# A spectral mixing block and a SwiGLU block under adaptive LayerNorm: a new order in the prologue, other PSUM banks for the last row transform, corrections by side copies, and the gate broadcast moved into the row loop

## The chip, the cores and the metric

The kernel runs on one core of a Trainium2 chip. A core has five engines with instruction queues of their own, each worked off in order: TensorE (PE, matrix products; its weight loads are listed as PEld), VectorE (DVE), ScalarE (ACT), GpSimd (POOL) and SyncE (SP, which here only issues DMAs). PE writes its results to PSUM, eight banks of 512 float32 in each of 128 partitions; DVE and ACT read them there. DMAs are issued from SP's, ACT's or POOL's queue. The metric is the device time of one execution in microseconds (us). A measurement is the median of several runs.

## The reference

One batch of 2048 rows (S) and 640 columns (D), in bfloat16. The model vector c gives six vectors of 640 through silu(c) @ w_mod: shift sa, scale ca and gate ga of the first half, sb, cb and gb of the second.

```python
def _A_ref(x, w_r, w_i):                     # spectral mixing
    X = rfft2(x, axes=(-2, -1))              # over rows and columns
    X = X * (w_r + 1j * w_i)
    return irfft2(X, s=(S, D)).astype(bfloat16)

def _B_ref(x, w_gate, w_up, w_down):
    return silu(x @ w_gate) * (x @ w_up) @ w_down      # inner width 1728

mod = (silu(c) @ w_mod).reshape(1, 6, 1, -1)
sa, ca, ga, sb, cb, gb = (mod[:, i] for i in range(6))
h = layernorm(x) * (1 + ca) + sa
x = x + ga * _A_ref(h, w_r, w_i)
h = layernorm(x) * (1 + cb) + sb
x = x + gb * _B_ref(h, w_gate, w_up, w_down)
```

## The kernel before

**Order.** The program is written in the order in which each engine is to run it; there is no scheduler. An engine that waits holds up all that stands behind it in its queue. SP's queue of DMAs is one list as well.

**Prologue (to about 15 us).** x comes in tiles of 128 rows, two (T = 2t, 2t + 1) to each of eight steps t. The column transform needs tables R (`Rp`, scaled by 1 + ca to `Rs`), the row transform tables `Gtab`. `bn(T)` takes mean and variance on DVE (two statistics instructions and an aggregate), `bn_act(T)` on ACT (two passes); `BA` (L341) lists the tiles that ACT takes. `rstd_of(t)` forms the variances on DVE (`vtmp`) and has POOL raise them to the power -1/2; `normed(t)` writes the two normalized tiles on DVE. `mod_cols` on PE gives ca, from which DVE forms `one_p_ca` and `m4c` and then, with POOL and ACT, the eight rows of `Rs`. `idle_pe` runs matmuls whose result is not used. `fetch(n)` issues n of 16 gathers from POOL's queue; they bring rows of the spectral weights w_i, w_r in reversed order into `Wt`.

**Row loop (L473, 15 to 38 us).** For each step, `tok(t)` multiplies the normalized tiles by `Gtab` (token product, banks 0 to 2), ACT copies the result (`Ys`), and `ddft(t)` multiplies it by `Rs` (banks 3 to 6); ACT copies that into `A_sb`. DVE and POOL prepare later steps meanwhile. At t = 5 `sa_cols`, at t = 7 `sa_rows` give the transform of the shift sa, and `sa_fix` its corrected form `FSA`, inside ddft(7). The copies of ddft(7) are split between DVE and ACT.

**Groups (38 to 69 us).** The 81 complex columns l are worked in 21 groups of up to four: 48 to 63 (groups 0 to 3), then {0, 80} (4), 1 to 47 (5 to 16), 64 to 79 (17 to 20). Groups 0 to 4 are transposed on PE (`t2_pe`), the others by four DMA transposes on SP (`t2_dma`). In each transposed block one column, index 0, needs a correction: `fix_in` multiplies it by the table TF, and DVE adds `FSA`. Then per group:
- `stage_a`: a PE product with KS2 per column, then two DVE products (`prod`, L574) with the spectral weights, for which `wsum` on POOL or DVE has formed a sum;
- `stage_b`: PE adds and transposes, ACT copies to `Y2`;
- `stage_c`, for units of one to three groups: PE multiplies by the inverse table KI; ACT (twice DVE) evicts into `Em` (columns below 64) or `Er`.

Index 0 of the second half is special again: for group 4 and the last six groups `row_col` has POOL copy it to `Zc`, and `stage_c` runs a second full matmul per column with KD. For the other columns `Y2c` collects index 0, and `row0` (L594) multiplies it by KI0, has ACT copy it (`E0c`) and SP store it into row 0 of `Em` by two small DMAs. Among the groups stand also the remaining model vectors: `ga_mod` (ga, broadcast to all partitions, `ga_bc`), and `mod_col` (sb, cb, gb; 25 matmuls of one column each), whose weights come by SP behind the transposes.

**Output rows (69 to 87 us).** For each of 16 tiles `s1em` and `s1er` on PE, a copy to `VT` on ACT, a PE product with RI (multiplied by ga; L1172, L1175), and on DVE the sum with x (`x1`, L1177). The second LayerNorm begins here: for the first two tiles `ln2_xn`, a DMA transpose on SP (`ln2_tr`, L777) and `ln2_mod` on POOL (L785), which applies cb and sb. The FFN weights come by SP, behind the two stores of row0: w_down (L722), two small pieces, then w_gate and w_up (L734). `gu13` (L989), the first product of the FFN, is on PE ahead of the last output tile.

**FFN (87 us to the end).** Four chunks of tiles, gate and up (L1001, L1031), then down (L879, L902).

Of the kernel before, what the change touches and what calls it, by code (L numbers as in the profile page):

```python
# [18 lines left out]
NT, P = 16, 128  # L19
# [68 lines left out]
def _tables():  # L88
# [28 lines left out]
    K = np.zeros((128, 832))  # L117
# [7 lines left out]
    K[:, 512:640] = C0 - Cr  # L125
# [48 lines left out]
def adaln_block_kernel(ctx, tc, A_x, A_w_r, A_w_i, B_x, B_w_gate, B_w_up, B_w_down, c, w_mod, out):  # L174
# [24 lines left out]
    Ktab = const.tile([P, 832], BF16, name="Ktab")  # L199
    KS2, KI, KB = Ktab[:, 0:192], Ktab[:, 192:320], Ktab[:, 320:384]  # L200
    TF, KD, KI0 = (Ktab[:, 384 + 128 * i:512 + 128 * i] for i in range(3))
    KDB = Ktab[:, 768:832]
    modcols = const.tile([P, 4, NC5], F32, name="modcols")
# [20 lines left out]
    FSA = const.tile([P, NL], F32, name="FSA")  # L224
# [9 lines left out]
    wm_r = rM.cut(12800, [NC5, 4, D])  # L234
# [14 lines left out]
    Zc = [rY.cut(4096 + 1024 * i, [4, 128]) for i in range(3)]  # L249
# [22 lines left out]
    nc.scalar.dma_start(Gtab[:, 0:2], Gd[:, 0:2])  # L272
    def load_x(xl, xh, gl, gh):
        nc.sync.dma_start(xh_sb[:, :, xl:xh, :], x_v[:, :, xl:xh, :])
        nc.sync.dma_start(Gtab[:, gl:gh], Gd[:, gl:gh])
# [4 lines left out]
    load_x(2, 3, 2, 6)  # L280
    nc.sync.dma_start(Rp[:, 0:4], R_dram[:, 0:4])
# [57 lines left out]
    if True:  # L339
        CS = (4, 0, 1, 2, 3)  # L340
        BA = (1, 3, 5, 11)  # L341

        def bn(T):
            for k in range(2):
                nc.vector.bn_stats(bn6a[:, k, :], x_sb[:, xslot(T), 320 * k:320 * k + 320])
            nc.vector.bn_aggr(mv[:, T, :], bn6a[:])
# [5 lines left out]
        def rstd_of(t):  # L352
            ts = slice(2 * t, 2 * t + 2)
            if 2 * t + 1 in BA:
# [6 lines left out]
            nc.gpsimd.tensor_tensor(rstd[:, ts], vtmp[:, ts], mhalf[:, 0:2], ALU.pow)  # L361

        def normed(t):
            for h in range(2):
                T = 2 * t + h
                nc.vector.tensor_scalar(XN[t % 3][h][:], x_sb[:, xslot(T), :], mv[:, T, 0:1], rstd[:, T:T + 1],
                                        ALU.subtract, ALU.mult)
# [14 lines left out]
        def ddft(t, mid=()):  # L382
            Ys = YS[t % 3]
            for ck in range(2):
                dft_d(banks(3 + 2 * ck, 2, [4, 256]), [Ys[:, CS.index(c5), 128 * ck:128 * ck + 128] for c5 in range(NC5)])
                if mid:
                    mid.pop(0)()
            for m in mid:
                m()
            Av = A_sb[:, :, t].rearrange("p l k c r -> p k c l r")  # L390
            av = banks(3, 4, [8, 256])[:, :, 0:RC].rearrange("p (k r) (c l) -> p k c l r", k=2, c=2)
            if t < NS - 1:
                nc.scalar.copy(Av, av)
            else:
                for ls in (slice(48, 64), slice(0, 48), slice(64, 81)):
                    for ck, cp in ((0, nc.vector.tensor_copy), (1, nc.scalar.copy)):
                        cp(Av[:, ck, :, ls], av[:, ck, :, ls])

        cps = psum[:, 7, 500:500 + NC5]
# [14 lines left out]
        fetch(2)  # L414
        bn(0)
        bn_act(1)
        rstd_of(0)
        bn(2)
        bn_act(3)
        fetch(1)  # L420
        normed(0)
        idle_pe(4)
        mps = psum[:, 7, 0:32 * NC5]
# [3 lines left out]
        idle_pe(3)  # L427
        mps = mps.rearrange("p (c w) -> p c w", w=32)[:, :, 0]
        rstd_of(1)
        nc.vector.tensor_scalar_add(one_p_ca[:], mps, 1.0)  # L430
        bn_act(5)
        nc.vector.tensor_scalar_mul(m4c[:], mask4[:], one_p_ca[:, 4:5])
        tok(0)
        for r in (1, 3):
            nc.scalar.mul(Rs[:, 0, r, :], Rp[:, r, :], one_p_ca[:, r:r + 1])
        normed(1)
        for r in range(2, 4):
            nc.gpsimd.tensor_scalar(Rs[:, 1, r, :], Rp[:, 4, :], m4c[:, r:r + 1], 1.0, ALU.mult, ALU.mult)
        for r in range(2):
# [3 lines left out]
        bn(4)  # L443
        fetch(1)
        rstd_of(2)
        fetch(2)
        bn(6)
        normed(2)
        idle_pe(2)

        def sa_cols():
            mps = psum[:, 7, 431:431 + NC5]
# [8 lines left out]
        def sa_rows():  # L461
            sps = psum[:, 7, 431:431 + NL]
# [5 lines left out]
        def sa_fix():  # L468
            fps = psum[:, 7, 431:431 + NL]
            nc.tensor.matmul(fps, lhsT=TF, rhs=SAb[:], start=True, stop=True)  # L470
            nc.vector.tensor_copy(FSA[:], fps)

        for t in range(1, NS):  # L473
            tok(t)
            if t < 6:
                (bn_act if 2 * t + 5 in BA else bn)(2 * t + 5)
                rstd_of(t + 2)
                if t < 5:
                    bn(2 * t + 6)
                normed(t + 2)  # L480
                fetch(1 + t % 2)
            ddft(t - 1)
            if t == 5:
                sa_cols()
                fetch(16)
            if t == 7:
                sa_rows()
        ddft(7, [sa_fix])
# [6 lines left out]
    if True:  # L495
        B2of = {}

        def t2_dma(bi):
# [4 lines left out]
            for i in range(n):  # L503
                B2of[l0 + i] = (B2b, i, l0, n)

        t2_dma(0)
        t2_dma(1)
        t2_dma(2)
        t2_dma(3)
        nc.sync.dma_start(wm_r[:, :, 1:3, :], wm_m[:, :, 1:3, :])  # L510
        nc.sync.dma_start(wm_r[:, :, 3, :], wm_m[:, :, 3, :])
# [3 lines left out]

        def fix_in(B2, n, fx, parts):
            nc.tensor.matmul(fx, lhsT=TF, rhs=B2[:, 0:n, 0], start=True, stop=True)
            for i0, i1, ls in parts:
                nc.vector.tensor_tensor(B2[:, i0:i1, 0], fx[:, i0:i1], FSA[:, ls], ALU.add)

        def t2_pe(slot):
            ls = groups[slot] + (groups[4] if slot == 3 else [])
            n = len(ls)
            tp = banks((0, 1, 6, 7)[slot], 1, [8, 128], BF16)
            for i, l in enumerate(ls):
                nc.tensor.transpose(tp[:, i, :], A_sb[:, l].rearrange("p t k c r -> p (t k c r)"), identb[:])
            B2 = (rM.cut(38400 + 1024 * slot, [n, 128]) if slot < 2 else rM.cut(10240 + 1024 * (slot - 2), [n, 128]))
            nc.scalar.copy(B2[:], tp[:, :n, :])
            for i, l in enumerate(ls):
                B2of[l] = (B2, i, None, None)  # L530

        def t2_fix(slot):
            B2, n = B2of[groups[slot][0]][0], 6 if slot == 3 else 4
            l0 = groups[slot][0]
# [775 lines left out]
```

## Time and profile before

| | us |
|---|---|
| median of 3 runs (lowest, highest) | 253.84 (253.65, 254.29) |
| the profiled execution's own time | 254.42 |
| its span, first to last instruction | 252.6 |
| to 10 us: PE busy | 5.83 of 10 |
| 10 to 38: PE, ACT, POOL busy | 24.00, 21.76, 20.04 of 28 |
| 38 to 69: PE, DVE, ACT busy | 28.91, 25.07, 23.88 of 31 |
| 69 to 87: PE busy | 17.82 of 18 |
| 87 to 253: PE busy | 162.21 of 166 |

A line of the timeline gives the start and the busy time in us, the engine (a q behind it stands for its queue, which issues a DMA), the line of the kernel, the operation, what it writes and reads with its shape, and how many instructions are merged. In brackets stands the time for which the engine was idle just before, and what ended that wait. A line of the windows gives a stretch of time, for each engine the busy time and the number of instructions, the granted PE clock (1.00 is full), the mean busy share of the DMA engines and GB/s. A line of the waits says who waited for whom: us in total, times, longest.

### The profile page before, as it was taken

How to read it: one execution, taken by the hardware profiler on the slowest of the kernel's cores; microseconds unless marked ns; L12 is line 12 of the kernel's file. 1: busy time of each engine (PE TensorE's matmuls, PEld its weight loads, DVE VectorE, ACT ScalarE, POOL GpSimd, SP SyncE). 2: the span in 40 equal slices, each digit the busy share in tenths (PEclk: the TensorE clock that was granted, in tenths of full speed). 3: DMA queues.
4: the chain of work that ended last, by engine and by line, in shares of the span. 5: the costliest groups of instructions: out<-in, count | busy, mean ns of one | idle time of the engine just before them, and what ended most of it. 6: DMA issues, size and time to landing. Idle time of an engine off the chain costs nothing.

```text
span 252.6 us, 5944 instructions
## 1 busy us (share of the span) xinstructions
PE 238.8 (95%) x2240; PEld 186.5 (74%) x2240; DVE 202.3 (80%) x493; ACT 171.1 (68%) x327; POOL 76.5 (30%) x111
## 2 busy tenths in 40 slices
PE   7587887999999999999999999999999999999994
PEld 2366866899989888778887778888675666656773
DVE  3695827997669999698998996778998788779964
ACT  5379876898689788858965387876247777774220
POOL 6675788671060633102001320000442000003410
PEclk9689999999999999999999999999999999999999
DMA  7999418998899999910001420300511000000111
GB/s 179 370 380 327 150 42 155 150 346 307 252 302 298 349 277 229 207 33 4 0 3 36 84 61 31 56 0 4 104 52 55 0 0 0 4 0 1 55 52 52
DMA packets 41310, 31.61 MB, mean 125 GB/s; under 512 B 22017, under 2 KB 37954, under 8 KB 41154
## 3 DMA queue, kind: packets, MB, share of 16 engines
q1 hardware_dynamic: 38704, 25.45, 36.9%
q0 software_dynamic: 2144, 5.58, 8.9%
q10 hardware_dynamic: 434, 0.21, 0.5%
q8 instruction: 17, 0.28, 0.5%
q14 instruction: 11, 0.09, 0.1%
HBM read 23.91 MB, written 2.62 MB: 105 GB/s over the span
## 4 chain that ended last, share of the span: by engine, by line
PE 83%; ACT 5%; DMA 3%; POOL 3%; DVE 2%; issue 2%; SPq 1%; DVEq 0%; ACTq 0%
PE psum L1031 35%; PE psum L902 19%; PE psum L1001 6%; PE psum L879 3%; DMA rM<-in_w_mod_dram 3%; PE psum L653 3%; PE psum L581 3%; PE psum L551 2%; PE psum L1172 2%; PE psum L1175 2%; PE psum L989 2%; POOL rW L336 2%; PE psum L377 1%; ACT rY L584 1%; PE psum L621 1%
## 5 line engine op out<-in xcount | busy, mean ns | idle before, releaser
L1031 PEld LDWEIGHTS <-rW 128*128 128x128 bf16 (+1 forms) x429 | 42.0, 98 | 12.6
L1031 PE MATMUL psum<-rW 128*128 128x256 bf16 (+1 forms) x247 | 42.2, 287 | 0.0
L928 POOL TENSOR_TENSOR rM<-rM,rL 128x320 f32<-128x320 f32 x6 | 5.4, 907 | 96.6 <-ACT rL L927 96.6
L902 PEld LDWEIGHTS <-rE 128*128 128x128 f16 (+1 forms) x196 | 19.0, 97 | 7.8
L902 PE MATMUL psum<-rE 128*128 128x320 f16 (+1 forms) x147 | 22.9, 299 | 0.0
L574 DVE TENSOR_TENSOR rM<-psum,rW 128x384 bf16<-128x384 f32 (+2 forms) x42 | 20.6, 547 | 2.1 <-PE psum L551 1.4
L1069 ACT COPY rX<-psum 128x384 f32<-128x384 f32 (+2 forms) x27 | 14.0, 519 | 7.3 <-PE psum L1031 7.2
L1062 ACT COPY rH<-psum 128x384 f32<-128x384 f32 (+2 forms) x27 | 13.9, 517 | 7.3 <-PE psum L1031 6.5
L1031 PEld LDWEIGHTS <-rE 128*128 128x128 f16 x156 | 15.2, 98 | 4.8
L1066 DVE TENSOR_TENSOR rH<-psum,rM 128x512 bf16<-128x512 f32 (+1 forms) x24 | 15.0, 624 | 4.4 <-PE psum L1031 2.6
L1085 ACT ACTIVATE rL<-psum 128x384 bf16<-128x384 f32 (+2 forms) x27 | 14.4, 532 | 5.4 <-PE psum L1031 3.4
L1070 DVE TENSOR_TENSOR rX<-psum,rX 128x384 f32<-128x384 f32 (+2 forms) x27 | 16.3, 604 | 1.7 <-ACT rX L1069 1.4
L1056 ACT COPY rM<-psum 128x384 f32<-128x384 f32 (+2 forms) x27 | 13.9, 515 | 4.0 <-PE psum L1031 3.9
L1031 PE MATMUL psum<-rE,rY 128*128 128x256 f16 (+1 forms) x78 | 15.6, 290 | 0.0
L1031 PE MATMUL psum<-rW,rE 128*128 128x256 bf16 (+1 forms) x78 | 15.6, 290 | 0.0
L1177 DVE SCALAR_TENSOR_TENSOR rM<-psum,rX 128x640 f32<-128x640 f32 x16 | 13.1, 821 | 2.7 <-ACT rL L657 1.4
L1086 ACT ACTIVATE rL<-rX 128x384 bf16<-128x384 f32 (+2 forms) x27 | 15.1, 558 | 0.0
L584 ACT CAST rY<-psum 128x512 bf16<-128x512 f32 (+2 forms) x21 | 11.8, 574 | 4.1 <-PE psum L581 3.7
L1001 PE MATMUL psum<-rW 128*128 128x256 bf16 x130 | 14.5, 273 | 0.0
L871 DVE TENSOR_TENSOR rA<-psum,rM 128x320 bf16<-128x320 f32 (+1 forms) x27 | 12.1, 472 | 2.4 <-PE psum L879 2.3
L1001 PEld LDWEIGHTS <-rW 128*128 128x128 bf16 x130 | 12.7, 98 | 1.6 <-issue 0.2
L1074 DVE TENSOR_TENSOR rH<-psum,rH 128x384 bf16<-128x384 f32 (+1 forms) x21 | 12.9, 615 | 0.0
(213 smaller groups left out, 641.7 us busy)
## 6 DMA issues: line engine op xcount, KB each, us to landing
out_dram<-rA SPq DMA_DIRECT2D x31, 80.0 KB
rM<-in_w_mod_dram SPq DMA_DIRECT2D x3, 800.0 KB
rA<-in_B_w_down_dram SPq DMA_DIRECT2D x2, 960.0 KB
rY<-in_B_w_gate_dram POOLq DMA_DIRECT2D x2, 832.0 KB
rM<-in_w_mod_dram SPq DMA_DIRECT2D x1, 1600.0 KB
rX<-in_A_x_dram SPq DMA_DIRECT2D x4, 320.0 KB
rX<-in_A_x_dram SPq DMA_DIRECT2D x2, 640.0 KB
rW<-in_B_w_gate_dram SPq DMA_DIRECT2D x2, 640.0 KB
```

Source lines behind the costliest of these rows:

```text
L574: nc.vector.tensor_tensor(PP[:, :, hl], xv[:, :, hl], in1, ALU.mult)
L584: nc.scalar.copy(Y2[:, 0:n, :], yps[:, 0:n, :])
L902: nc.tensor.matmul(o, lhsT=lhs[rows(k), k], rhs=rhs[rows(k), k], start=start and k == ks[0], stop=stop and k == ks[-1], skip_group_check=True)
L1001: nc.tensor.matmul(gu[u], lhsT=Wgu[:, u, c5, ff * 128:(ff + 1) * 128], rhs=h2T[:, :, c5, :], start=(c5 == 0), stop=(c5 == NC5 - 1))
L1031: nc.tensor.matmul(o[:, f], lhsT=w, rhs=b, start=(start and f == 0 and i == 0), stop=(stop and f == len(groups[g]) - 1 and i == len(ops) - ...
L1056: nc.scalar.copy(c0, X)
L1062: nc.scalar.copy(c2, X)
L1066: nc.vector.tensor_tensor(c11, Z, c0, ALU.add)
L1069: nc.scalar.copy(c3, X)
L1070: nc.vector.tensor_tensor(c22, Y, c3, ALU.add)
L1085: nc.scalar.activation(g21, X, ACT.Silu, scale=-1.0)
L1086: nc.scalar.activation(g22, c22, ACT.Silu, scale=-1.0)
```

## The change

**Prologue.** Tile 0's and tile 1's variances are formed and raised to the power separately. tok(0) goes ahead of ca's `mod_cols`, which stands behind it. `BA` is cut to tiles 1 and 3; DVE takes tiles 5 and 11. DVE's order becomes: normed(1), bn(4), one_p_ca, Rs, bn(5). In SP's queue Rp's four rows and two tiles of Gtab go ahead of the third x load. POOL forms no row of Rs any more, writes `sc_rep` at the start, and issues its gathers in a new order: one before tok(0), four behind, two before the loop, then two, two, two and three in steps 1 to 4. `fetch(3)` at t = 5 finds none left.

**Row loop.** bn and normed change their order and distance. `ddft` uses banks 4 to 7, and for t = 7 banks 0 to 3; the copies of ddft(6) are split between DVE and ACT as well. At t = 7 DVE forms `wsum` of columns 48 to 63, and the two `ga_mod` run on PE around ddft(6), with their copies on DVE. `sa_rows` stands behind ddft(7); `sa_fix` and `FSA` go.

**Groups.** The correction of index 0 adds the shift inside PSUM, by a second matmul with TF. For the blocks transposed on PE, DVE copies index 0 to a side tile `Bc` first, and ACT copies the rest. Group 5 is transposed on PE as well. For the blocks from the DMA transposes the correction runs two groups ahead, and ACT copies it back, behind the products. `Zc`, its memset and `row_col` go: the second matmul of `stage_c` writes only output partition 0, and for groups 17 and 18 `col0` corrects index 0 by two small matmuls with KM and an ACT copy, so that they need no second matmul. sb, cb and gb are formed at groups 14, 16 and 18, 25 matmuls each, and `row0` at group 19, with two ACT copies. The last two units run ahead of `s1em(0)` and `s1em(1)`. `wsum` on POOL is earlier. `wm_r` is laid out with the vector outermost, and its last three parts are loaded one by one.

```diff
-    K = np.zeros((128, 832))
+    K = np.zeros((128, 960))
...
-    K[:, 512:640] = C0 - Cr
+    K[:, 512:640] = C0 @ np.linalg.inv(Cr)
+    K[:, 832:960] = C0 - Cr
...
+    KM, KD = KD, Ktab[:, 832:960]
...
+    nc.sync.dma_start(Rp[:, 0:4], R_dram[:, 0:4])
+    nc.sync.dma_start(Gtab[:, 2:4], Gd[:, 2:4])
...
-    load_x(2, 3, 2, 6)
-    nc.sync.dma_start(Rp[:, 0:4], R_dram[:, 0:4])
+    load_x(2, 3, 4, 6)
...
-        BA = (1, 3, 5, 11)
+        BA = (1, 3)
...
-        def ddft(t, mid=()):
+        def ddft(t):
             Ys = YS[t % 3]
+            zb = [banks(4 + 2 * ck, 2, [4, 256]) for ck in range(2)]
+            if t == NS - 1:
+                zb = [banks(0, 2, [4, 256]), banks(2, 2, [4, 256])]
             for ck in range(2):
-                dft_d(banks(3 + 2 * ck, 2, [4, 256]), [Ys[:, CS.index(c5), 128 * ck:128 * ck + 128] for c5 in range(NC5)])
...
+                dft_d(zb[ck], [Ys[:, CS.index(c5), 128 * ck:128 * ck + 128] for c5 in range(NC5)])
...
+        def ga_mod(lo, bank):
+            gps_ = mod_bc(0, lo, bank)
+            nc.vector.tensor_copy(ga_bc[:, :, lo // 4:lo // 4 + 80], gps_.rearrange("p (m r) -> p r m", r=4))
+
+        def mods(i, mps):
+            for c5 in range(NC5):
+                mod_col(mps[:, c5:c5 + 1], wm_r[:, :, i], c5)
+            if i == 2:
+                return lambda: nc.vector.tensor_scalar_add(one_p_cb[:], mps, 1.0)
+            return lambda: nc.vector.tensor_copy(modcols[:, 2 + i // 2, :], mps)
...
         nc.gpsimd.memset(SL[:], 0.0)
-        fetch(2)
+        nc.gpsimd.tensor_copy(sc_rep[:], sc_f[:].unsqueeze(2).to_broadcast([P, NC5, 128]))
         bn(0)
+        rstd_of(0, 0)
         bn_act(1)
-        rstd_of(0)
-        bn(2)
+        bn(2, True, False)
+        rstd_of(0, 1)
+        fetch(1)
+        normed(0, (0,))
+        bn(2, False, True)
+        normed(0, (1,))
         bn_act(3)
-        fetch(1)
-        normed(0)
-        idle_pe(4)
-        mps = psum[:, 7, 0:32 * NC5]
+        idle_pe(6)
+        tok(0)
+        rstd_of(1)
+        fetch(4)
+        mps = psum[:, 3, 0:32 * NC5]
         mod_cols(mps, wm_ca, range(0, 3), 32)
         idle_pe(1, 2)
         mod_cols(mps, wm_ca, range(3, 5), 32)
-        idle_pe(3)
+        idle_pe(2)
         mps = mps.rearrange("p (c w) -> p c w", w=32)[:, :, 0]
-        rstd_of(1)
+        normed(1)
+        bn(4)
         nc.vector.tensor_scalar_add(one_p_ca[:], mps, 1.0)
-        bn_act(5)
...
-        tok(0)
...
+        bn(5)
         rstd_of(2)
         fetch(2)
-        bn(6)
-        normed(2)
-        idle_pe(2)
...
         for t in range(1, NS):
             tok(t)
             if t < 6:
-                (bn_act if 2 * t + 5 in BA else bn)(2 * t + 5)
+                bn(2 * t + 4)
+            if t < 7:
+                normed(t + 1)
+            if t < 6:
+                bn(2 * t + 5)
                 rstd_of(t + 2)
                 if t < 5:
-                    bn(2 * t + 6)
-                normed(t + 2)
-                fetch(1 + t % 2)
-            ddft(t - 1)
+                    fetch(2 + t // 4)
             if t == 5:
                 sa_cols()
-                fetch(16)
+                fetch(3)
             if t == 7:
-                sa_rows()
-        ddft(7, [sa_fix])
+                for hl in range(2):
+                    wsum(48, 64, nc.vector, hl)
+            if t == 7:
+                ga_mod(0, 3)
+            ddft(t - 1)
+        ga_mod(320, 3)
+        ddft(7)
+        sa_rows()
...
-        nc.sync.dma_start(wm_r[:, :, 1:3, :], wm_m[:, :, 1:3, :])
-        nc.sync.dma_start(wm_r[:, :, 3, :], wm_m[:, :, 3, :])
+        for i in range(1, 4):
+            nc.sync.dma_start(wm_r[:, :, i, :], wm_m[:, :, i, :])
...
-        def fix_in(B2, n, fx, parts):
-            nc.tensor.matmul(fx, lhsT=TF, rhs=B2[:, 0:n, 0], start=True, stop=True)
+        def fix_in(col, fx, o, parts, cp):
+            n = col.shape[1]
+            nc.tensor.matmul(fx, lhsT=TF, rhs=col, start=True, stop=False, skip_group_check=True)
             for i0, i1, ls in parts:
-                nc.vector.tensor_tensor(B2[:, i0:i1, 0], fx[:, i0:i1], FSA[:, ls], ALU.add)
+                nc.tensor.matmul(fx[:, i0:i1], lhsT=TF, rhs=SAb[:, ls], start=False, stop=i1 == n, skip_group_check=True)
+            return lambda: cp(o, fx)
...
-            nc.scalar.copy(B2[:], tp[:, :n, :])
+            o = 4 * slot + 2 * (slot == 3)
+            nc.vector.tensor_copy(Bc[:, o:o + n], tp[:, :n, 0])
+            nc.scalar.copy(B2e[:, o:o + n, 1:128], tp[:, :n, 1:128])
...
+            bf = blk_fix(g + 2, b0) if g > 2 else lambda: None
+            post = [bf]
+            mi = {14: 1, 16: 2, 18: 3}.get(g)
+            if mi:
+                post.append(mods(mi, psum[:, b0, 224:224 + NC5]))
+            if g == NG - 2:
+                post.append(row0(psum[:, b0 + 1, 192:256]))
...
+        def col0(g, fx):
+            for i in range(2):
+                nc.tensor.matmul(fx[:, 4 * i:4 * i + 4], lhsT=KM, rhs=Y2s[g + i][:, :, 0], start=(i == 0), stop=(i == 1))
...
-                        nc.tensor.matmul(o, lhsT=Zc[g % 3][:, i, :], rhs=ks[1], start=False, stop=True)
+                        nc.tensor.matmul(o[0:1], lhsT=Y2[:, i, 0:1], rhs=ks[1], start=False, stop=True, skip_group_check=True)
...
         t2_pe(0)
         t2_pe(1)
-        t2_pe(2)
         t2_fix(0)
-        wsum(48, 64, nc.vector, 0)
+        t2_pe(2)
         t2_pe(3)
-        t2_fix(1)
-        wsum(48, 64, nc.vector, 1)
-        PPs[0] = stage_a(0)
-        ga_mod(320, 5)
+        PPs[0] = stage_a(0, lambda: t2_fix(1))
...
-            if g == NG - 5:
-                row0(2)
-            if g == NG - 1:
-                for c5 in range(NC5):
-                    mod_col(psum[:, 3, 192 + c5:193 + c5], wm_r[:, :, 3], c5)
         s1em(0)
-        stage_c(len(units) - 2)
-        evac(len(units) - 2)
...
         s1em(1)
-        stage_c(len(units) - 1)
-        evac(len(units) - 1)
```

## The prediction

> **What bounds the kernel now.** Shares first, then the chain of waits to see where TensorE (PE) does not set the pace, then the timeline of those places.
>
> ```profile
> PE 238.8 (95%) x2240; PEld 186.5 (74%) x2240; DVE 202.3 (80%) x493; ACT 171.1 (68%) x327; POOL 76.5 (30%) x111
> PEclk9689999999999999999999999999999999999999
> ```
>
> PE is busy 95%. The list of PE's waits from 69 us on has one entry:
>
> ```profile
> PE psum L663 <- ACT rE L630: 0.5, 1, 0.5
> ```
>
> So this change can only act before 70 us, unless it makes something late for a later stage. Up to 38 us, PE waits in the row loop. POOL there, then the loop's last step:
>
> ```profile
> 17.49 0.73 POOL L361 TENSOR_TENSOR rstd<-vtmp,mhalf 128x2 f32<-128x2 f32 x1
> 18.41 1.18 POOL L336 DMA_INDIRECT rW<-in_A_w_i_dram,ridx  x1 [0.19 <-issue]
> 19.89 0.95 POOL L336 DMA_INDIRECT rW<-in_A_w_i_dram,ridx  x1 [0.31 <-issue]
> 20.86 0.72 POOL L361 TENSOR_TENSOR rstd<-vtmp,mhalf 128x2 f32<-128x2 f32 x1
> ```
> ```profile
> 31.96 0.81 DVE L366 TENSOR_SCALAR rE<-rX,mv,rstd 128x640 bf16<-128x640 bf16 x2 [0.83 <-POOL rstd L361]
> ```
> ```profile
> 32.80 1.25 PE L377 MATMUL psum<-rE 128*128 128x256 bf16 x10 [0.20 <-DVE rE L366]
> ```
>
> One pow and two gathers cost POOL 20.86 - 17.49 = 3.37 us (3.20 at 25.11). The last pow (31.21) gives the last normed tile and tok(7) at 32.80. From 42 to 66 us PE, DVE and ACT are nearly full together. Then comes a chain that crosses queues:
>
> ```profile
> 61.98 1.26 SPq L599 DMA_DIRECT2D rE<-rY  x2
> 63.34 1.12 SPq L722 DMA_DIRECT2D rA<-in_B_w_down_dram  x2
> ```
> ```profile
> 64.00:64.50 0.50, 0.50 (x12) 0.50 (x10) 0.39 (x4) 0.06 (x1) 0.20 (x1) 1.00 0.05 2
> 80.00:80.50 0.50, 0.50 (x10) 0.46 (x8) 0.50 (x1) 0.50 (x2) 0.00 (x0) 1.00 1.61 339
> 81.50:82.00 0.50, 0.50 (x9) 0.46 (x8) 0.50 (x3) 0.50 (x3) 0.00 (x0) 1.00 0.33 26
> ```
> ```profile
> 83.50 2.42 POOL L785 TENSOR_SCALAR rW<-rW,one_p_cb,modcols 128x256 bf16<-128x256 bf16 x4 [7.38 <-DMA rW<-rL]
> ```
> ```profile
> 85.86 0.71 PE L989 MATMUL psum<-rW,Wp 128*128 128x256 bf16 x5
> ```
>
> SP issues the two row-0 stores (L599) and only behind them the FFN weights. The last column of the windows is GB/s: nothing flows at 64, 339 to 407 up to 80.5, then the transposed load L777 (issued at 77.25) drains until 82, and POOL gets it at 83.50. POOL ends at 85.92, and gu13 (L989), which needs it, runs at 85.86 to 86.57, 0.71 instead of some 0.55 us: it was paced by POOL. That chain has about 0.1 us to spare.
>
> **The change, part by part.** All against the profiled execution: span 252.6, its own time 254.42. The difference is then put on the median of the runs, 253.84, which is 0.6 under that time.
>
> 1. *Prologue.* tok(0) goes ahead of the modulation columns. That alone frees no later step, because ddft(0) needs Rs, and Rs needs one_p_ca. On DVE bn(4) now stands ahead of one_p_ca and waits for the third x tile, which in SP's queue is moved behind Rp (162 KB) and two G tiles (128 KB). Before, that tile landed at 11.4 (ACT's wait, L349). The next 256 KB landed 0.45 us later and Rp 0.5 after that (the issues of SP that waited on them: 11.89, 12.35), so 290 KB cost 0.5 + 0.25; by the mean flow of 0.37 MB/us it is 0.8. Two gathers fewer by then give back about 0.2: landing 12.0 (bounds 11.4 to 12.6). Then bn 1.15, one_p_ca and m4c 0.4, five Rs 1.0 (0.18 to 0.26 each, L442), bn(5) 1.15, vtmp 0.2: the pow for step 2 starts at 15.9. Here ddft(0) comes near 14.6, 1.6 us earlier than in the trace (16.19), but the gain is not kept, by the next point. The moves that cost nothing: sc_rep (0.74) to POOL's idle front, Rs' third row to ACT (0.37) and off POOL (2 x 0.48), two more idle matmuls, 32 KB more Ktab; each sits in time in which its engine waits for the third x tile.
>
> 2. *Row loop.* bn_act(5) and (11) go from ACT (4 x 0.93 = 3.7 us) to DVE (2 x 1.15). ACT is no longer the pace; DVE needs 2 x 1.15 + 0.1 + 0.72 = 3.1 us a step. POOL needs more: all 16 gathers now stand ahead of the last pow, where 12 stood. From 15.9: four steps of 3.3, then a pow and three gathers, 0.73 + 0.2 + 3 x 1.26 = 4.6: the last pow at 33.7. pow 0.73 and two normed 0.75: tok(7) at 35.1 instead of 32.80, +2.3. Even if POOL never idled from its first gather (7.6 us), 16 x 1.27 + 6 x 0.93 = 25.9 put that pow at 33.5 less the 1.4 of idle I count, 32.5, and tok(7) at 34.0. So +1.2 to +3.1.
>
> The Trainium skill, "SBUF", section "Who interferes with whom", speaks against the change here: a DVE instruction in a two-port mode fully blocks POOL on the shared port. In the rows, a gather that starts beside a normed pair (21.77, 29.23, 32.13) takes 1.17 to 1.19, one alone (16.51, 19.89) 0.95, so 0.2, not a whole 0.8. By the rule each step would be up to 0.6 longer and tok(7) 3 us later still; I keep the rows, where that 0.2 is already inside the 3.3.
>
> 3. *From tok(7) to the products.* tok 1.25, first ga_mod 5 x 0.14 = 0.69, ddft(6) 1.1, second ga_mod 0.69, ddft(7) 1.1 in its own banks (the 0.61 us wait for ACT at 36.56 is gone), sa_rows 0.56: PE free at 40.5. Transposes, Bc copies and the first fix: first product on DVE at 42.65 against 40.90. But two wsum (0.98), the fixes between the first products (four waits of 0.2 to 0.7) and ga_mod no longer stand among them: product 3 ends at 46.85 against 45.63, group 6 starts on PE at 48.05 against 46.98. Of the 2.3 lost, 1.1 is left. ga_mod and wsum cost nothing more only because DVE was going to wait there; wsum waits for the last gather (36.3), still before DVE's share of ddft(6) at 37.6.
>
> 4. *Steady groups.* A pair of groups is 2 x (0.33 + 0.45 + 0.22) = 2.0 us on PE and also in the trace (evictions L632 at 54.24, 56.24, 58.28). The fixes go from DVE (4 x 0.23) to ACT (4 x 0.2) and cost an extra tiny matmul each: I take 0, bounds -0.5 (the waits of PE on L519) and +0.5 (ACT is in the chain of waits from 53.7 to 59). The 75 one-column matmuls (0.024 each, 25 in 0.60) stand at groups 14, 16, 18, so all 1.8 us precede the end of group 16; 20 did before. +1.3 there. Their weights come in three loads of 800 KB where one of 1600 and one of 800 were. In the trace the four transposes move data from 40 to 49, then w_mod, H and RI from 50 to 62. All of it goes 2.1 later with the first transpose (A copied at 40.65 instead of 38.58), so the three land near 55, 57 and 59, ahead of their use at 57, 60 and 62. That cover is 2 to 3 us; what it lacks PE would wait.
>
> 5. *Tail.* From the end of the products' unit (13, 14) to the first output row (L1172): 60.5 to 69.80, 9.3 us. After: two stage_a 0.66, row0 0.15, four stage_b 1.8, unit (15, 16) 0.9, col0 and its ACT copy 0.4, units (17, 18), 19, 20 at 0.45 each 1.35, s1em 0.9 + 0.35, and ACT's last VT copy 0.3: 6.8, with 0.3 for waits 7.1. -2.2. Gone are 55 column matmuls, 8 of the doubled ones, the wait on L630 and Zc's POOL copies and its memset (1.46), which bounded nothing.
>
> PE alone: +1.1 + 1.3 - 2.2 = +0.2 at the first output row.
>
> 6. *What is late next.* Row-0's copy is queued on ACT behind the eviction of unit (13, 14), in both kernels. That unit ends 1.1 + 1.3 later, so the copy and SP's stores are some 2.3 us later (64.3 instead of 61.98), and the weights behind them too (65.6 instead of 63.34). The flow to 80.5 is full, so the transposed load lands 2.2 later, 85.7, POOL ends at 88.1, and gu13, which PE reaches at 86.0, waits 2.1 us. Behind it PE has no waits in which this could vanish. Whole: about +2.1, of which the +0.2 of PE is part. 253.84 + 2.1 = 255.9. Its own range, by +1.2 to +3.1 at tok(7) and half a microsecond in the groups: 254.8 to 257.1.
>
> **The rivals.**
> - *Nothing is waited for at gu13 (even).* Speaks for it: the transposed load was issued at 77.25 and might need its 6 us for other reasons than the queue; PE's own sum then stands, +0.2: 254.0. Against: the flow is at 339 to 407 GB/s until it drains.
> - *Faster.* POOL's gathers run without the gap of 0.3 and the third x tile lands at 11.4, so tok(7) comes by 33.9, 1.2 earlier; PE's sum is then -1.0, with the fixes' waits saved -1.5: 252.3. The late weights would still cost 2.3 - 1.2 - 0.1 = +1.0, so it also needs 1 to 2 us of slack there that the trace hides. For it: the tail's 2.2 us are counted from single rows. Against: 16 gathers in order ahead of the last pow.
> - *Much slower.* After tok(1) PE idles some 2 us for Rs. In the trace, after 3 us of idle from 5.86, the granted clock was 0.65 at 8 to 9 us and 0.50 until 15. A loop at half clock has 2 x 2.4 = 4.8 us a step against 3.3; two such steps add 3.0, on top of the late weights 258.9. A step fills PE more than half, and a gap of 1.5 us at 24 us left the clock at 1.00, so I give it little.
>
> The Trainium skill, "TensorE: Matmul & The Clock Gate", section "Part 1: The HAM clock gate", has the clock halved after one idle window of some 3.4 us. In this trace it fell at 8.3, 2.4 us after PE's last matmul, so the measured time is shorter than the page's. By the page a gap of 2 us costs nothing, by the row it is just short of a drop.
>
> **How the numbers follow.** Late weights 0.56, even 0.18, faster 0.20, half clock 0.06. The time is that of the first, 255.9. What a measurement can tell from no change is 0.3%, 0.76 us. Faster than 253.1: the faster rival, 0.20; within: the even one and nothing else, 0.18; slower: the rest, 0.62. The range reaches down to the middle of the faster rival and up past the first's end: 252.7 to 257.3.
>
> **What would show it.** Step 1: bn(4) starts near 12.0 and one_p_ca behind it. Step 2: three gathers ahead of the last pow, tok(7) near 35.1; at 33 or below the step is wrong. Step 3: first product near 42.6. Step 5: from unit (13, 14) to the first output row about 7.1 us. Step 6: row-0 stores near 64.3, gu13 waiting with POOL's modulation as the releaser; if PE shows no wait there, the forecast is wrong by 2 us.

## The result, and the profile after

| | before | after |
|---|---|---|
| median of 4 runs (lowest, highest), us | 254.06 (253.65, 254.30) | 260.06 (259.88, 260.41) |
| ratio, 95% interval | | 1.0239 (1.0219 to 1.0260) |
| the profiled execution, its span, us | 254.42, 252.6 | 259.89, 258.1 |

The change makes the kernel 6.0 us slower. The forecast, 255.9, had the side right and the size wrong: 260.06 lies above its range. First the shares and the granted clock from the page of the changed kernel, then three lines from its list of PE's waits (who waited, for whom, us in total, times, longest):

```profile
PE 242.3 (94%) x2243; PEld 187.4 (73%) x2243; DVE 207.0 (80%) x495; ACT 167.4 (65%) x324; POOL 73.5 (28%) x102
PEclk9999979999999999999999999999999999999999
```
```profile
PE psum L387 <- DVE rE L376: 7.1, 8, 1.8
PE psum L585 <- DVE rE L551: 0.7, 1, 0.7
PE psum L548 <- DMA rL<-rA: 0.4, 1, 0.4
```

Three things are to be seen. PE is busy for 3.5 us more with as many matmuls as before (2243 against 2240). The clock, which was low at the start before, is low in the sixth slice instead, where the row loop ends. And the forecast's new wait, gu13 behind POOL (L1002), is nowhere in the whole list. The waits of L387 are the POOL-paced row loop, as forecast.

Set side by side, the times of the same work in the two timelines (us; starts, where nothing else is said) show where the time went:

| | before | after | later by | forecast |
|---|---|---|---|---|
| tok(7) ends | 34.05 | 35.49 | 1.4 | 2.3 |
| first product on DVE | 40.90 | 42.98 | 2.1 | 1.75 |
| group 6 on PE | 46.98 | 48.54 | 1.6 | 1.1 |
| first stage_a behind group 4's unit | 51.09 | 54.22 | 3.1 | 1.1 |
| unit (13, 14) | 60.04 | 64.69 | 4.65 | 2.4 |
| first output row | 69.80 | 75.36 | 5.6 | 0.2 |
| gu13 | 85.86 | 91.45 | 5.6 | 2.1 |
| end of the span | 252.6 | 258.1 | 5.5 | 2.1 |

Everything is lost before 75 us. The largest miss of the forecast is in the tail, between unit (13, 14) and the first output row, where a gain of 2.2 stood in the forecast and 0.9 was lost. Unit (15, 16) of the changed kernel, first two columns (start, us, engine, line, operation):

```profile
66.75 0.22 PE L664 MATMUL psum<-Ktab,rY 128*128 128x128 bf16 x1
66.90 0.22 PE L666 MATMUL psum<-Ktab,rY 128*1 128x128 bf16 x1
67.05 0.23 PE L664 MATMUL psum<-Ktab,rY 128*128 128x128 bf16 x1
67.21 0.22 PE L666 MATMUL psum<-Ktab,rY 128*1 128x128 bf16 x1
```

and the same two columns of the kernel before:

```profile
63.22 0.22 PE L621 MATMUL psum<-Ktab,rY 128*128 128x128 bf16 x1
63.28 0.22 PE L623 MATMUL psum<-Ktab,rY 128*128 128x128 bf16 x1
63.34 0.22 PE L621 MATMUL psum<-Ktab,rY 128*128 128x128 bf16 x1
63.39 0.22 PE L623 MATMUL psum<-Ktab,rY 128*128 128x128 bf16 x1
```

The durations are alike, 0.22; they overlap, so what counts is the distance from start to start. It is 0.056 before and 0.155 after, for the one-column matmul (128*1) and for the full one behind it alike. The weight loads (PEld) differ in the same way. First two of the changed kernel, then two of the kernel before:

```profile
66.90 0.08 PEld L666 LDWEIGHTS <-rY 128*1 128x1 bf16 x1
67.05 0.10 PEld L664 LDWEIGHTS <-rY 128*128 128x128 bf16 x1
```
```profile
63.23 0.10 PEld L623 LDWEIGHTS <-rY 128*128 128x128 bf16 x1
63.28 0.10 PEld L621 LDWEIGHTS <-rY 128*128 128x128 bf16 x1
```

Before, a load starts 0.01 behind the start of the matmul ahead of it (63.22) and 0.05 ahead of its own matmul (63.28). After, it starts 0.15 behind the matmul ahead of it (66.75) and together with its own (66.90). Why the load no longer goes ahead, no run shows.

The second loss is the clock behind tok(7); in these windows of the changed kernel the third number from the end, ahead of DMA share and GB/s, is the granted clock:

```profile
35.00:35.50 0.50, 0.50 (x5) 0.38 (x3) 0.31 (x1) 0.00 (x0) 0.45 (x2) 0.57 0.00 0
35.50:36.00 0.50, 0.50 (x3) 0.30 (x2) 0.00 (x0) 0.42 (x1) 0.50 (x1) 0.50 0.00 0
38.50:39.00 0.50, 0.50 (x6) 0.42 (x5) 0.34 (x1) 0.16 (x1) 0.50 (x2) 1.00 0.00 0
```

The mean of 0.57 in the first window puts the fall at 35.1; the clock is back at 38.5, so it was halved for 3.4 us. PE had waited 1.77 us for the last normed tiles until 33.69, and another 0.22 between the two.

Three theories were tested. **S**: the switch between a 128-column and a 1-column weight costs 0.1 us each way. **C**: the wait ahead of tok(7) makes the clock fall. **W**: the forecast's late weights are there, but hidden: row-0 stores at 67.03 (61.98 before), w_down at 68.34 (63.34), POOL's modulation 89.22 to 91.60 (83.50 to 85.92), all 5.0 to 5.7 late, and PE is as late itself.

### The profile page after: what moved, and what is told of

Same layout as the page of the kernel before. It is cut to its first block, busy times and chain, and to the rows that moved or that the text cites. A ratio compares the mean times of both kernels' runs of the same rounds, so it can differ in the third digit from the quotient of the medians.

```text
span 258.1 us, 5948 instructions
## 1 busy us (share of the span) xinstructions
PE 242.3 (94%) x2243; PEld 187.4 (73%) x2243; DVE 207.0 (80%) x495; ACT 167.4 (65%) x324; POOL 73.5 (28%) x102
## 4 chain that ended last, share of the span: by engine, by line
PE 81%; DMA 7%; POOL 6%; DVE 2%; issue 2%; ACT 1%; SPq 0%; DVEq 0%
PE psum L1044 35%; PE psum L915 18%; PE psum L1014 6%; POOL rW L338 4%; DMA rX<-in_A_x_dram 4%; PE psum L892 3%; PE psum L685 3%; DMA rL<-rA 3%; PE psum L664 2%; PE psum L615 2%; PE psum L1185 2%; PE psum L1188 2%; POOL rstd L371 2%; PE psum L1002 2%; PE psum L585 2%
## 5 line engine op out<-in xcount | busy, mean ns | idle before, releaser
L1044 PEld LDWEIGHTS <-rE 128*128 128x128 f16 x156 | 15.3, 98 | 4.7
L387 PE MATMUL psum<-rE 128*128 128x256 bf16 x80 | 11.5, 277 | 7.4 <-DVE rE L376 7.1
L387 PEld LDWEIGHTS <-rE 128*128 128x128 bf16 x80 | 8.0, 111 | 10.9 <-DVE rE L376 10.9
L390 ACT CAST rE<-psum 128x1280 bf16<-128x1280 f32 x8 | 9.8, 1223 | 8.9 <-PE psum L387 8.9
```

The costliest lines, as they stand in the source:

```text
L387: nc.tensor.matmul(Y[:, s, :], lhsT=lhsT, rhs=Gtab[:, 2 * t + h, :], start=(h == 0 and s % 2 == 0), stop=(h == 1 and (s % 2 == 1 or s == 4 ...
L1044: nc.tensor.matmul(o[:, f], lhsT=w, rhs=b, start=(start and f == 0 and i == 0), stop=(stop and f == len(groups[g]) - 1 and i == len(ops) - ...
```

## The experiments

Each time is the median in us. The kernel before, measured beside each group of runs, took 253.7 to 254.2.

**1. All columns (S, W).**

```diff
-    nc.tensor.matmul(o[0:1], lhsT=Y2[:, i, 0:1], rhs=ks[1], ...)
+    nc.tensor.matmul(o, lhsT=Y2[:, i, :], rhs=ks[1], ...)
```

> The changed kernel with the second matmul of stage_c given all 128 columns as weights and all 128 output partitions (so the KD product is added to every row of the second half, not to row 0 alone; the values of the affected groups differ from the reference). Theory S (alternating between a 128-column and a 1-column weight makes every matmul of the pair 0.155 instead of 0.056): the 18 pairs shrink from 0.31 to 0.11, 3.6 us of PE; the tail from unit (13, 14) to the first output row falls from 10.2 to 7.1 and the first output row comes at 71.8 instead of 75.36. Theory W (behind that, the first FFN product is held by POOL's modulation, whose data stand in SP's queue behind the row-0 stores; those gain only the 0.4 us of group 4): PE then waits some 3 us at gu13 and the time is only 259.4 to 259.9. S without W: 256.5. Rival (the pairs are slow for another reason, PSUM accumulation or the bank): the pairs stay at 0.31 and the time at 260.1.

259.42. The pairs take 0.11:

```profile
65.04 0.22 PE L664 MATMUL psum<-Ktab,rY 128*128 128x128 bf16 x1
65.09 0.22 PE L666 MATMUL psum<-Ktab,rY 128*128 128x128 bf16 x1
65.15 0.22 PE L664 MATMUL psum<-Ktab,rY 128*128 128x128 bf16 x1
```

From the end of unit (13, 14) to the first output row it is 7.4 us (63.43 to 70.86); the forecast had 7.1. PE then waits at gu13, as W says, though 2.0 and not 3; the line of the waits of this run:

```profile
PE psum L1002 <- POOL rW L798: 2.0, 4, 1.2
```

By the median, 3.6 us of PE were taken out and 0.6 came out at the end. The trace is of the fastest of the five executions, 258.17 at a mean clock of 0.991. There the first output row comes 4.5 earlier than in the changed kernel, since besides S this execution has no fall of the clock behind tok(7). At the end 1.7 of this are left (259.89 to 258.17); the rest goes mostly into the wait. The other four executions took 259.32 to 259.72 at mean clocks of 0.980 to 0.984; no trace shows where their clock was low.

**2. Row-0 stores from ACT's queue (W), and with edit 1.**

```diff
-    nc.sync.dma_start(E0r[:, :, ls], E0c[:, ls])
+    nc.scalar.dma_start(E0r[:, :, ls], E0c[:, ls])
```

> The changed kernel with the two row-0 stores issued from ACT's queue, so that SP issues the FFN weights without waiting for row 0. W: the weights start near 63 instead of 68.3, POOL's modulation ends by 89 instead of 91.6, but PE reaches gu13 only at 91.4, so the time moves by -0.3 to 0: 259.8 to 260.1. Rival L (the late weights are the main cost, as the prediction had it): gu13 comes 2 us or more earlier, 258.0 or less.

> Both of the above together (same values left different as in the first). S and W: neither alone gives much, together they give the whole 3.4: 256.6, no wait at gu13. If W is wrong, the time is that of the first of the two within 0.4.

266.44 and 265.88: far slower than either theory had it. The first FFN weights are now issued before 58 us, and the second store is issued only at 73.74. The timeline of ACT in the first of the two runs, in brackets the idle time and its releaser:

```profile
65.57 0.54 ACTq L633 DMA_DIRECT2D rE<-rY  x1
73.74 0.48 ACTq L633 DMA_DIRECT2D rE<-rY  x1
74.31 1.07 ACT L618 CAST rY<-psum 128x512 bf16<-128x512 f32 x2 [7.99 <-DMA rA<-in_B_w_down_dram]
```

ACT stood 8 us until a w_down load had landed. The pair says nothing on W; why that issue waits for that load was not settled.

**3. Idle matmuls ahead of tok(7) (C).**

```diff
     for t in range(1, NS):
+        if t == 7:
+            for i in range(7):
+                nc.tensor.matmul(banks(3, 1, [512]), lhsT=ones[:], ...)
         tok(t)
```

> The changed kernel with seven more idle matmuls of 512 columns (about 1.5 us) ahead of tok(7), in the 1.8 us in which PE waits for the last normed tile. Theory C (that wait is what made the granted clock fall to 0.50 from 35.2 to 38.5, which costs half of 3.3 us): the clock stays at 1.00, the first product comes at 41.4 instead of 42.98, all of it is carried to the end since the row-0 stores move with it: 258.4 to 258.7. Rival (the last copies of A and the transposes' 7 us set the pace of the first groups, and a faster ddft(6) is waited away): 259.8 to 260.1, with more wait at the first products.

258.47 (258.42 to 258.93): C's number, 1.6 less. From the first matmul of tok(7) to the first product it takes 7.63 us here (34.26 to 41.89), and 9.29 in the changed kernel (33.69 to 42.98). So the fall of the clock costs 1.7.

That the wait brings the fall is not shown by this. Runs 1, 2 (the first) and 7 kept the wait (1.97, 1.98 and 1.52), and their traces have no fall behind tok(7): 7.63 to 7.64 as well. The changed kernel, run 2 (the second) and runs 4 and 5 had waits of 1.77 to 1.97, the fall, and 9.1 to 9.3. With the wait filled or shortened (this run and the four of 8, below) no trace has it there; the last of these has it at 42.8, behind other waits. So it came in four of seven traces with the wait and in none of five without it.

In this run's trace the clock fell as well, but from 15.3 to 22.1, inside the loop that POOL paces, and that cost little: the four executions agree within 0.5 at mean clocks from 0.987 to 1.000.

**4. KI ahead of KD in each group (S).**

```diff
-    if col: nc.tensor.matmul(o[0:1], lhsT=Y2[:, i, 0:1], rhs=ks[1], ...)
+    if col: late.append((o[0:1], Y2[:, i, 0:1], ks[1]))
+ for o, l_, r_ in late:
+    nc.tensor.matmul(o, lhsT=l_, rhs=r_, ...)
```

> The changed kernel, but in each group of stage_c first all matmuls with KI, then all one-column matmuls with KD. S (a switch between the two shapes costs 0.1 each way): a group of four has 2 slow matmuls instead of 8, 2 x 0.155 + 6 x 0.056 = 0.65 instead of 1.24 us, 2.6 us of PE less in all. Theory N (the one-column matmul is slow by itself): 5 x 0.155 + 3 x 0.056 = 0.94 a group, 1.3 us less. The time shows little of either, since by W gu13 then waits: 259.5 to 260.0.

260.05, at the edge of what was expected, with 1.8 us of wait at gu13. The rows of this run decide between S and N:

```profile
66.72 0.39 PE L665 MATMUL psum<-Ktab,rY 128*128 128x128 bf16 x4
67.03 0.38 PE L669 MATMUL psum<-Ktab,rY 128*1 128x128 bf16 x4
67.35 0.40 PE L665 MATMUL psum<-Ktab,rY 128*128 128x128 bf16 x4
```

A group of four pairs takes 67.35 - 66.72 = 0.63; S had 0.65, N 0.94. Four one-column matmuls in a row are as fast as four full ones; only the alternation is slow.

**5. 64 columns (S).** As edit 1, with `o[0:64]` and `Y2[:, i, 0:64]`.

> The changed kernel with 64 columns as weights and 64 output partitions in the second matmul (rows 1 to 63 of the second half then get a KD product too, other values in those groups). S: 64 columns are as much another shape as one column, a pair stays at 0.31. Theory N' (the price falls with the number of columns loaded, by way of the last output partitions): a pair near 0.2. The time says little (259.5 to 260.1); the rows decide.

260.36 (two executions), and a pair still takes 0.32 or a little more:

```profile
66.87 0.22 PE L664 MATMUL psum<-Ktab,rY 128*128 128x128 bf16 x1
67.02 0.24 PE L666 MATMUL psum<-Ktab,rY 128*64 128x128 bf16 x1
67.19 0.23 PE L664 MATMUL psum<-Ktab,rY 128*128 128x128 bf16 x1
```

So N' falls: 64 columns cost no less than one. Other widths were not tried, and the width of the weight and the number of output partitions change together in all of these runs, so which of the two counts stays open.

**6. The one-column matmul in the kernel before (S alone).**

```diff
-    nc.tensor.matmul(o, lhsT=Zc[g % 3][:, i, :], rhs=ks[1], ...)
+    nc.tensor.matmul(o[0:1], lhsT=Zc[g % 3][:, i, 0:1], rhs=ks[1], ...)
```

> The kernel before, with one edit: its 26 second matmuls with Zc use only column 0 as weights and write only output partition 0. Nothing else moves. S: each pair goes from 0.11 to 0.31, 26 x 0.2 = 5.2 us of PE, with no cover: 258.8 to 259.4. If the slow pairs of the changed kernel come from something else in it, the time stays at 254.1.

260.67, more than S alone: +7.0. One of the four executions took 258.17 (+4.5, below S's 5.2) at a mean clock of 0.992, the others 260.5 to 261.3 at 0.978 to 0.979. The trace is of the slowest, and its windows at the place show what was added there:

```profile
70.50:71.00 0.50, 0.50 (x5) 0.30 (x4) 0.00 (x0) 0.46 (x1) 0.00 (x0) 1.00 1.08 364
71.50:72.00 0.50, 0.50 (x6) 0.50 (x6) 0.33 (x1) 0.00 (x0) 0.00 (x0) 0.50 1.27 185
77.50:78.00 0.50, 0.50 (x7) 0.50 (x6) 0.28 (x2) 0.29 (x1) 0.15 (x1) 0.54 1.07 338
78.00:78.50 0.50, 0.50 (x9) 0.42 (x7) 0.00 (x0) 0.30 (x1) 0.50 (x2) 1.00 0.62 193
```

From 63.25 on PE works mostly on such pairs (0.31 each), and at 71.1 the clock halves for 6.8 us, with PE busy 0.50 of 0.50 in each window and no wait over 0.2 in its list.

**7. All columns, and the first w_down load early (W).**

```diff
     PPs[2] = stage_a(2)
+    load_wd(0)
```

> The run with 128 columns in the second matmul (same values left different), and the first of the two large w_down loads emitted behind stage_a(2), which puts it ahead of the row-0 stores in SP's queue, in the stretch from 64.5 to 70 us in which nothing flows. W: POOL's modulation ends some 2.5 us earlier, the 2.0 us of wait at gu13 go, and the time falls from 259.4 to 257.2. If the modulation is late for another reason (its own transposed load, or POOL), the time stays at 259.4 within 0.4.

255.63: W is shown. POOL's modulation in run 1, then in this run:

```profile
87.51 2.21 POOL L798 TENSOR_SCALAR rW<-rW,one_p_cb,modcols 128x256 bf16<-128x256 bf16 x4 [10.36 <-DMA rW<-rL]
```
```profile
84.62 2.48 POOL L801 TENSOR_SCALAR rW<-rW,one_p_cb,modcols 128x256 bf16<-128x256 bf16 x4 [7.23 <-DMA rW<-rL]
```

It ends at 87.10 instead of 89.72, 2.6 earlier (2.5 expected). The wait at gu13 is gone from the list, and PE reaches it at 87.13 (88.16 in run 1 with a wait, 91.45 in the changed kernel). The two traced executions, both without a fall of the clock behind tok(7), differ by 2.5 (258.17 and 255.63), near W's 2.2. The medians differ by 3.8, but four of run 1's five executions had a lower clock than its trace. With S out and W mended, 1.95 of the 6.0 us are left.

**8. The gathers (step 2 of the prediction), and all mends together.**

```diff
-    fetch(2 + t // 4)
+    fetch(2)
```

> The changed kernel with two gathers instead of three between the last two pows on POOL; the sixteenth goes behind the last pow. Theory P (POOL's gathers set when tok(7) starts): last pow at 31.2 instead of 32.42, tok(7) 1.2 earlier, PE's wait ahead of it 0.6 instead of 1.8; with C the clock then does not fall behind it either. DVE's wsum waits for the last gather, some 1 us, ahead of its copy of ga. First product 1.0 (P alone) to 2.6 (P and C) earlier, 257.4 to 259.0. Rival (DVE's bn and normed pace the loop, or wsum's new wait gives it back): tok(7) moves by less than 0.4, 259.7 to 260.3.

259.15. The last pow comes at 31.66, tok(7) 0.7 earlier (33.03): the gathers do pace it, by half of P's 1.2. In this trace the clock does not fall behind it. But the first product comes at 42.46, against 42.98 in the changed kernel and 41.89 in run 3. DVE in this run, wsum:

```profile
36.77 0.96 DVE L333 TENSOR_TENSOR rW<-rW 128x512 bf16<-128x512 bf16 x2 [3.29 <-DMA rW<-in_A_w_r_dram,ridx]
```

wsum waits for the sixteenth gather, and behind it stands ga's copy (37.61), for which PE waits 1.6.

The next two have the mends of runs 3, 4 and 7, compute what the changed kernel computes, and have col0 also for groups 15 and 16 (`if g == NG - 4: col0(NG - 6, psum[:, 4, 192:200])()`); the second has this gather order as well.

> The changed kernel with S, C and W mended at once and all values right: KI matmuls ahead of KD matmuls in each group, groups 15 and 16 corrected by col0 as 17 and 18 are (no second matmul), seven idle matmuls ahead of tok(7), the first large w_down load ahead of the row-0 stores. Against the run with 128 columns and the early load (255.6): group 4 and the last two groups 0.2 each slower, units (15, 16) 0.45 faster, the clock's fall at 35 excluded: 255.0 to 255.8.

> The same with the gather order of the first of these runs, and three idle matmuls instead of seven. P: 1.0 to 1.2 less than the run beside it, 254.0 to 254.7. If the gathers do not set the pace, no difference.

257.31 and 257.41. The added col0 made a wait of its own, 1.6 us in both: its sums lay in bank 4, which the next stage_a needs, behind ACT's copies. P's gain does not show in the second, which has the 1.6 us wait for ga's copy again. A third run moved the sums to bank 2 and `wsum` between the corrections:

> The changed kernel, all values right: KI ahead of KD in each group, col0 for groups 15 and 16 too (its sums in bank 2, which no later stage_a needs), the first large w_down load early, two gathers for three ahead of the last pow, and wsum of columns 48 to 63 moved from the row loop to between the corrections of the first transposes, so that DVE does not wait for the sixteenth gather ahead of its copies. Theory P' (gathers set tok(7), and wsum's wait was what gave the 1.1 us back): against the earlier run with all mends (257.3) the wait of 1.6 on ACT's copy in bank 4 and 1.1 at tok(7) go: 254.4 to 254.9. If the first groups are bound by the transposed blocks instead: 255.6.

257.83. P' falls: tok(7) is early (32.89), but wsum, now 1.21 and 1.39 us a half instead of 0.48, stands ahead of the correction, for which PE waits 1.7 and 0.8, and the clock falls there (42.8 to 46.2). What is left of the loss was not found in the row loop in this way.

**9. The tail's part alone, on the kernel before.** Groups 15 to 18 by col0 instead of Zc, with and without the early load:

> The kernel before with two things alone: groups 15 to 18 are corrected by col0 (KM, two small matmuls and two ACT copies a pair of groups) in place of Zc and the second matmul, and the first large w_down load goes ahead of the row-0 stores. 16 matmuls of 0.056 go, 0.9 us of PE, less 0.1 for the small ones and 0.3 for a wait on ACT's copy as in the changed kernel. W: with the early load gu13 does not take it back: 253.2, 0.5 less than before. If the edit brings a wait of its own: 254.0 or more.

> The same without the early load. W: PE comes 0.5 earlier to gu13, whose data come no earlier, so the time is that of before within 0.2: 253.7. If the late load is no bound here: 253.2 as in the run beside it.

255.70 with, 254.15 without (ratio to the kernel before 1.0021, 1.0007 to 1.0035). Without it the 0.9 of matmuls went into two waits of col0 (0.67 for DVE in the bank it shares, 0.3 for ACT); the remaining 0.4 or so was not explained. With the load early, the row-0 stores lie behind it; two waits of that run from 60 to 75:

```profile
PE psum L665 <- DMA rE<-rY: 1.1, 1, 1.1
PE psum L602 <- DVE rM L580: 0.7, 1, 0.7
```

What helped the changed kernel (its stores came at 67) hurts here, where they come at 61.4: PE waits 1.1 for them. The trace is of the slowest of nine executions (257.17; the fastest took 254.69), and its clock also falls, from 67.8 to 71.1. A last run put row0 ahead of unit (13, 14)'s eviction and the last two units ahead of s1em(0):

> The kernel before with col0 for groups 15 to 18 as in the two runs before this, but: col0's first sums in bank 6 (free until the unit that needs them), row0 ahead of unit (13, 14) so that its copy on ACT goes ahead of that eviction, and the last two units ahead of s1em(0), as the changed kernel has them. W: the row-0 stores are issued some 0.8 us earlier, so the FFN weights and POOL's modulation too; PE saves 16 x 0.056 and the 0.45 us wait for the last eviction, less 0.4 for col0: 252.8 to 253.3, up to 0.9 less than before. If the modulation is held by something else than the row-0 stores, gu13 waits and the time stays at 253.7 to 254.1.

259.11. The eviction writes row 0 of its eight columns too, so it now waits 3.81 us for the stores and, done after them, overwrites these values. The trace has this wait, and 3.5 us of PE behind it, so the run says nothing on W:

```profile
65.32 1.01 ACT L644 CAST rE<-psum 128x1024 bf16<-128x1024 f32 x1 [3.81 <-DMA rE<-rY]
```

No version tried here beats the kernel before.

## Why the prediction was wrong, point by point

1. *Prologue.* The mechanism was right (bn(4) first, then one_p_ca), the landing not: 10.80 instead of 12.0, below my lower bound of 11.4. The 290 KB put ahead of it do not show in its landing (11.4 before, 10.8 after); what made up for them was not tested. The pow came at 14.61 instead of 15.9, ddft(0) at 12.75 instead of 14.6.
2. *Row loop.* Right: the pows lie 3.23 to 3.38 apart (3.3), the last 4.46 (4.6). With the earlier start tok(7) began 1.4 before the forecast (33.69 against 35.1) and ended 0.9 before it. That, and step 1, were errors in the change's favour. Three slips in the working did not decide this. 33.5 less 1.4 is 32.1, not 32.5, so the lower bound at tok(7) was +0.8 and not +1.2. 0.73 + 0.2 + 3 x 1.26 is 4.7, not 4.6. And beside a normed pair a gather takes 1.01 to 1.19, not 1.17 to 1.19: those at 15.16 and 26.02 took 1.05 and 1.01.
3. *From tok(7) to the products.* Here the half-clock rival, held at 0.06, came true in another place. I looked for a fall in the loop, where PE idles at each step, and priced tok(7) to the first product at full clock: 7.55 us, which is right without the fall (7.63) and 1.7 short with it (9.29). Ahead of tok(7) step 2 had itself made a longer wait, 4.46 instead of 3.3 us for the last step, 1.8 us of PE. That this wait set off the fall is argued: four traces of seven with it have the fall.
4. *Steady groups.* 0 was taken, with ±0.5. The mods were nearly right: 1.5 between 54.22 and 64.69, 1.3 forecast. Between 48.54 and 54.22 another 1.6 were lost, three times the bound: 0.4 are the two pairs of group 4 (S); the list of waits has 0.4 for the transposed block, issued 2.7 later, 0.3 for an eviction of ACT and 0.2 for products; the remaining 0.4 are in no entry of it. These were seen, not tested. Run 7, without S, still loses 1.1 in this stretch.
5. *Tail.* **This is the step that failed.** It took "unit (15, 16) 0.9" and "units (17, 18), 19, 20 at 0.45 each", which is the trace's 0.056 a matmul carried over to a shape that the trace did not have. Unit (15, 16) took 2.47 and the last two units together 2.48: 16 x 0.2 = 3.2 us. Everything else in the step held: run 1, without the switch, has 7.4 for the forecast's 7.1. The trace of the kernel before has no matmul with one weight column among full ones, so this term needed a bound on both sides; it was costed as if it were the old matmul made smaller. Runs 1, 4, 5 and 6 show what stood in its place: 0.1 us for each switch of the weight's width. The Trainium skill, "TensorEngine Tiling (Array Packing)", section "Tiling Modes", "Key Properties", says that changing the tiling mode, and not just the tile, drains TensorE. Whether a weight of 1 or 64 columns counts as another mode, no run here shows.
6. *What is late next.* Runs 1 and 7 show that this bound exists: the weights are late, POOL's modulation too, and gu13 is where they meet PE. But in the changed kernel PE was 5.6 late itself and did not wait there. So the 2.1 us of the forecast came from a wait that did not happen, and that the change came out slower, as forecast, is luck: PE's own sum, which the forecast had at +0.2, made it so.

In sum, at the first output row the forecast had +0.2 and the trace +5.6. Of the 5.4 between, 3.1 are the tail (S gives 3.2), 1.6 the stretch of step 4 (0.4 of it S), and 0.2 the mods. The other 0.5 lie ahead of group 6: tok(7) began 1.4 earlier than forecast, the fall of the clock cost 1.7, and some 0.2 are spread over the first groups.

## What to carry to other kernels

A matmul cut down to fewer weight columns was not cheaper here but dearer, because it alternated with full ones. Either keep the shape, or put all of one shape together, and read such a change from start-to-start distances, not from the duration column. Work put ahead of the last wait of a loop can cost twice if the wait grows: once itself, and once more if the clock falls behind it. And two chains that end at the same instruction have to be shortened together; in the trace of run 1, PE was 4.5 us earlier and 1.7 came out at the end.

## What the runs showed of the hardware

- One switch between a 128-column weight and a 1- or 64-column weight costs 0.1 us, on both matmuls of the pair: 0.155 from start to start instead of 0.056 (0.15 to 0.18 with 64 columns). A run of four one-column matmuls has the full rate but for its first (run 4). At a switch the weight load starts together with its matmul instead of 0.05 ahead.
- The granted clock halved although the profile shows PE full: in run 6 after 8 us that were mostly pairs of 0.31 us, which take 0.11 without the switch. In the changed kernel it halved 3.2 us after PE went idle (31.92), with 2.0 us of this idle and tok(7) under way. The Trainium skill, "TensorE: Matmul & The Clock Gate", section "Part 1: The HAM clock gate", names at least one idle window of about 3.4 us as the condition; neither case here had one, and the measurement decides.
- Traces of the same row loop had the fall between 34 and 39 (the changed kernel, the second of run 2, run 5), between 15 and 22 (runs 1, 7 and the first of run 2), or at both places (run 4). In the loop that POOL paces it moved tok(7) by under 0.5 us (33.98 to 34.10 against 33.69 to 34.04); behind it, it cost 1.7.
